# A small GpSimd step between any two indirect DMAs of a sorted-attention kernel

## The chip, the cores and the metric

The kernel runs on one core of one Trainium2 chip. A core has five engines that each work through a queue of their own, in order: PE (matrix products; its weight loads are shown apart as PEld), DVE (vector work), ACT (activation functions and copies), Pool (GpSimd: small general steps, and here every indirect DMA) and SP, which only issues DMAs. Engines wait for each other and for DMAs through semaphores.

The metric is the time of one execution on the device in microseconds (us), the median of several runs.

## The reference

Clustered attention over 4 batches, 8 heads, 768 tokens and a head size of 64, and behind it a small feed-forward network (FFN) over the 3072 tokens. A query attends only to the keys whose nearest of 16 centroids is its own nearest:

```python
q_assign = np.argmax(np.einsum('bhsd,hcd->bhsc', q_n, c_n), axis=-1)
k_assign = np.argmax(np.einsum('bhsd,hcd->bhsc', k_n, c_n), axis=-1)
mask = q_assign[:, :, :, None] == k_assign[:, :, None, :]
scores = scale * np.matmul(q, k.transpose(0, 1, 3, 2))
scores = np.where(mask, scores, -1000000000.0)
...
out = np.matmul(softmax(scores), v)

x = out.transpose(0, 2, 1, 3).reshape(B * S, H * D)
h = np.maximum(np.maximum(x @ w1, x @ w2), x @ w3)
return h @ w_out
```

Here `q_n`, `k_n` and `c_n` are the vectors divided by their lengths; `w1`, `w2`, `w3` are 512 x 768 and `w_out` is 768 x 512.

## The kernel before

Since a query meets only the keys of its own cluster, the kernel sorts the tokens of each head by cluster and computes attention in eight blocks of 128 places (`NJ = 8`, `NPLACE = 1024`). A place is a row of a buffer in DRAM, and the sorting of keys and values is done by DMA with computed addresses.

For each of the 32 heads (batch `b`, head `h`) the work goes through these steps:

- `four_units` (lines 367 to 493) finds clusters and places for four heads at a time: PE scores the centroids, DVE picks the best and counts, and the place of each token ends as an integer in the tile `cl_idx`.
- `split_kv` (line 548) makes 16-bit halves of keys and values in the tile `kv` (ACT at line 554, DVE at line 555).
- `scatter` (line 573) sends these rows to their places in a buffer in DRAM, one of a ring of four (`ring`, the name `kv_` in the code, `kv` in the profile). It takes six indirect DMAs, one for each 128 tokens, issued by Pool at line 578. No wait stands between the six, but each waits for the last readers of the ring's buffer.
- `read_back` (line 595) loads the sorted keys (a transposing DMA at line 602) and values (line 603) on SP's queue; they wait for all six scatters.
- `order_q` (line 615) sorts the queries on PE with products by 0/1 matrices: DVE builds `hot` at line 622, PE multiplies at line 624.
- `scores` (line 648) computes the blocks on PE and their exponentials on ACT (line 665), makes halves on DVE (line 670) and transposes them by DMA (line 672). `values` (line 678) multiplies with the values and writes the sorted result `of` to one of four buffers in DRAM (`oring`, the name `o`), with a DMA of SP at line 691.
- `gather` (line 693) brings the rows back in token order: six indirect DMAs of Pool at line 699 from `o` into `xb`, which holds one batch and has one buffer (`NXB = 1`). They wait for the write at line 691, and for `xb` to be free.

When the eight heads of a batch are gathered, `x_split` (line 713) makes halves of `xb` on ACT and DVE and transposes them by DMA into `x16`. The FFN of that batch (`ffn_units`, hidden products at line 741, output products at line 774) is spread over the steps of the next batch's heads. The FFN of the last batch has no next batch and runs alone at the end. The FFN weights are converted during the first twelve heads (`w_units`, `wo_units`).

The order is not written out by hand. Each piece of work gets a priority in `plan` (lines 792 to 863): for head number k, the scatter is put at k - 2.5, the read back at k - 1.5, the scores at k, the values at k + 0.5 and the gather at k + 1.6. When the program is built, a scheduler goes through the instructions with a time estimate of its own and fixes one order for each engine, so Pool's queue holds groups of six scatters and groups of six gathers. Behind the setup of tables and constants, Pool's queue holds nothing else.

Behind this program stands a second one, `every_pair__attn__then__maxout_ffn`, that runs only where the sorting does not fit its buffers. The profile has no work of it.

Of the kernel before, what the change touches and what calls it, by code (L numbers as in the profile page):

```python
# [8 lines left out]
F32 = mybir.dt.float32  # L9
# [6 lines left out]
ALU = mybir.AluOpType  # L16
# [7 lines left out]
def sorted_attn__then__maxout_ffn(  # L24
# [17 lines left out]
    nc = tc.nc  # L42
# [3 lines left out]
    P = 128  # L46
# [27 lines left out]

    def const(shape, dt, name):
        return cpool.tile(shape, dt, name=name)

    def after(x, o, why=mybir.DependencyReason.DATA):
        tc.add_manual_dep(
            x.ins, o.ins.name, mybir.DependencyInfo(mybir.DependencyClass.Sync, why), reason="one of several places"  # L80
        )


    ident = const([P, P], F32, "ident")
    make_identity(nc, ident)
    ident16 = const([P, P], BF16, "ident16")
    nc.gpsimd.tensor_copy(ident16, ident)
    identh = const([P, P], F16, "identh")
    nc.gpsimd.tensor_copy(identh, ident)
    cw = const([P, H, 2 * C], F32, "cw")  # L90
    nc.gpsimd.memset(cw, 0.0)

    def table(shape, name, *tests, dt=F16, fill=0.0):

        t = const([P] + shape, dt, name)
        nc.gpsimd.memset(t, 1.0)
        for free, part, base in tests:
            nc.gpsimd.affine_select(
                out=t, in_=t, pattern=[[f, n] for f, n in zip(free, shape)], compare_op=ALU.is_ge, fill=fill, base=base,
                channel_multiplier=part,  # L100
            )
        return t
# [27 lines left out]
    first = table([4, NJ, 4], "first", ([-2 * C, 0, 0], 1, 0), ([2 * C, 0, 0], -1, 2 * C - 1))  # L130
# [11 lines left out]
    side = const([P, 4], F32, "side")  # L142
# [356 lines left out]
    def pair_units(b, pr):  # L499
# [67 lines left out]
        def index(h, n, u):  # L567
            a = 2 * (2 * (pr & 1) + h) + u
            return fours[b, pr // 2]["idx"][:, n, a : a + 1]
# [3 lines left out]
        def scatter(h):  # L573
            def f():
                at = (2 * g + h) % NRING
                sent = d["sent", h] = []
                for n in range(QT):
                    i = nc.gpsimd.indirect_dma_start(  # L578
                        out=ring[at],
                        out_offset=bass.IndirectOffsetOnAxis(ap=index(h, n, 1), axis=0),  # L580
                        in_=d["kv", h][:, n].rearrange("p a d -> p (a d)"),
                        in_offset=None,
                        bounds_check=NPLACE - 1,
                        oob_is_err=False,
                    )
                    for o in sent:
                        tc.declare_no_dep(i.ins, o.ins, reason="each place is one token's")
                    for o in ring_last[at]:
                        after(i, o, mybir.DependencyReason.ANTI)
                    sent.append(i)  # L590
                ring_last[at] = []

            return f
# [99 lines left out]
    def gather(b, h):  # L693
        d, i = st[b, h // 2], h & 1
        od = oring[(b * H + h) % NOUT]
        if b not in xb:
            xb[b] = sb.tile([P, QT, DM], F32, tag="xb", name="xb", bufs=NXB)
        for n in range(QT):
            nc.gpsimd.indirect_dma_start(  # L699
                out=xb[b][:, n, h * D : h * D + D],  # L700
                out_offset=None,
                in_=od,
                in_offset=bass.IndirectOffsetOnAxis(ap=d["index"](i, n, 0), axis=0),
            )

    x16, xsc = {}, {}

# [125 lines left out]
    for b in range(B):  # L833
        for h in range(H):
            k = b * H + h
            put(k, when(k, k), scores, b, h)
            put(k + 1, when(k + 0.5, k), values, b, h)
            put(min(k + 1 + LATE, B * H), when(k + 0.6 + LATE, k), gather, b, h)
        k = b * H + H + LATE
        if b + 1 < B:  # L840
            put(k + 1, k - 0.5, x_scale, b)
            for n in range(QT):
                put(k + 1, k - 0.5 + 0.01 * n, x_split, b, n)
            units = [u for gi in range(NG) for u in ffn_units(b, gi)]
            spread(units, k + 1, k + H + 1 + (F2 if b == 2 else 0), 0)
# [778 lines left out]
```

## Time and profile before

| | before |
|---|---|
| median of 3 runs | 772.13 us (768.11 to 774.67) |
| the profiled execution, whole | 773.91 us |
| its span, first to last instruction | 772.2 us |
| mean granted TensorE clock | 0.885 of full |
| indirect DMAs | 192 scatters (L578), 192 gathers (L699) |

The span is what the views of the profile divide up; the execution has 1.7 us around it. L578 is line 578 of the kernel. A busy time counts only the time in which an engine works on an instruction; an engine's idle time ahead of an instruction is listed with what ended it, and `issue` stands for idle time in which the engine waited for nothing that the profile shows. For an indirect DMA the busy time is that of Pool, which makes the DMA's addresses, and not that of the transfer. Views group instructions by line and form (out<-in by names of tiles, partitions x elements, type), list the waits, or give the order of time.

The two groups of indirect DMAs are, with busy us, the mean ns of one, and the idle time ahead of them with what ended it:

```profile
L699 POOL DMA_INDIRECT xb<-o,cl_idx x192 | 195.5, 1018 | 132.8 <-DMA o<-of 70.5 <-issue 53.3 <-DVE xh L274 5.6
L578 POOL DMA_INDIRECT kv<-kv,cl_idx x192 | 212.5, 1107 | 85.0 <-issue 51.5 <-DVE kv L555 28.0 <-DMA xb<-o,cl_idx 0.9
```

Together Pool is busy with them for 408 us and idle ahead of them for 218 us, of which `issue` is 105 us.

### The profile page before, as it was taken

Reading aid. Unit: us, or ns where it says so; the run is one execution under the profiler, and the core shown is the slowest. Engines: PE = TensorE matmul, PEld = TensorE weight load, DVE = VectorE, ACT = ScalarE, POOL = GpSimd, SP = SyncE. Lnnn points to the kernel's source line nnn. Section 1 sums busy time; section 2 is a strip of 40 time slices with the busy share of each in tenths; the row PEclk is TensorE's granted clock in tenths of the full one; section 3 lists DMA queues with packets and bytes.
Section 4 is the critical chain, followed back from the end, with each engine's and each line's share of the span. In section 5 each row is a group of like instructions: output and inputs, shape, how many; then the busy total and the mean of one; then the engine's idle time right before and its main releaser. Section 6 shows DMA issues by size and latency. Waiting matters only on the chain.

```text
span 772.2 us, 12828 instructions
## 1 busy us (share of the span) xinstructions
PE 621.5 (80%) x4284; PEld 352.6 (46%) x4313; DVE 473.8 (61%) x1202; ACT 410.9 (53%) x978; POOL 426.4 (55%) x478
## 2 busy tenths in 40 slices
PE   3466446566527899999999998988799999999993
PEld 1233223334314465555455655644366465564651
DVE  4787867887588888586769765775554324121220
ACT  2567665977585666564867655565644413211111
POOL 6374577777765467777767575767276544000000
PEclk8579756557658899999999999999899999999998
DMA  9778879999699567898976656477845434200001
GB/s 319 272 214 188 224 179 221 271 220 255 180 265 184 138 144 204 172 217 172 215 172 162 130 135 176 118 154 138 163 90 113 120 77 84 69 1 28 14 1 46
DMA packets 231197, 120.54 MB, mean 156 GB/s; under 512 B 200656, under 2 KB 209872, under 8 KB 231120
## 3 DMA queue, kind: packets, MB, share of 16 engines
q1 hardware_dynamic: 218832, 100.72, 55.1%
q0 software_dynamic: 12288, 18.90, 9.7%
q8 instruction: 36, 0.59, 0.3%
q14 instruction: 41, 0.34, 0.1%
HBM read 58.75 MB, written 29.36 MB: 114 GB/s over the span
## 4 chain that ended last, share of the span: by engine, by line
PE 42%; DMA 15%; issue 13%; POOL 12%; DVE 9%; ACT 6%; SPq 2%; POOLq 0%; DVEq 0%; ACTq 0%
PE one L741 24%; PE one L774 9%; POOL kv L578 6%; POOL xb L699 5%; PE big L624 4%; DMA kv<-kv,cl_idx 4%; DMA xb<-o,cl_idx 3%; ACT e L665 2%; DMA o<-of 2%; DMA x<-xh 2%; DVE hot L622 2%; DMA wd<-in_moe_w_dram 1%; DVE kv L555 1%; DMA kt<-kv 1%; PE big L656 1%
## 5 line engine op out<-in xcount | busy, mean ns | idle before, releaser
L741 PE MATMUL one<-x,w 128*128 128x384 f16 x1728 | 296.6, 329 | 12.4 <-DVE wf_h L753 4.0
L699 POOL DMA_INDIRECT xb<-o,cl_idx x192 | 195.5, 1018 | 132.8 <-DMA o<-of 70.5
L578 POOL DMA_INDIRECT kv<-kv,cl_idx x192 | 212.5, 1107 | 85.0 <-issue 51.5
L741 PEld LDWEIGHTS <-w 128*128 128x128 f16 x1728 | 168.8, 99 | 126.7 <-issue 20.1
L624 PE MATMUL big<-hot,q 128*128 128x512 f16 x384 | 122.9, 442 | 47.9 <-DVE q L565 19.8
L665 ACT ACTIVATE e<-big,nm,sc_al 128x128 f32<-128x128 f32 x256 | 113.6, 462 | 29.2 <-DVE nm L661 16.2
L622 DVE TENSOR_SCALAR hot<-line,cl_code 128x1024 f16<-128x1024 f16 x192 | 92.3, 498 | 5.5 <-PE big L624 5.1
L624 PEld LDWEIGHTS <-q 128*128 128x128 f16 x384 | 37.6, 107 | 92.7 <-issue 46.9
L753 DVE SCALAR_TENSOR_TENSOR wf_h<-one,wf_h 128x384 f32<-128x384 f32 x48 | 26.6, 554 | 55.4 <-PE one L741 55.3
L753 DVE SCALAR_TENSOR_TENSOR vf_h<-one,vf_h 128x384 f32<-128x384 f32 x48 | 26.7, 555 | 51.0 <-PE one L741 51.0
L665 ACT ACTIVATION_READ_ACCUMULATOR e<-big,nm,sc_al 128x1 f32 x256 | 53.4, 209 | 0.0
L774 PE MATMUL one<-wo,wf_h 128*128 128x512 f16 x216 | 49.3, 386 | 1.5 <-ACT o L783 0.8
L774 PE MATMUL one<-wo,vf_h 128*128 128x512 f16 x216 | 48.7, 379 | 1.4 <-ACT o L783 1.4
L660 DVE TENSOR_REDUCE nm<-big 128x8 f32<-128x1024 f32 x32 | 39.0, 1217 | 16.0 <-PE big L658 8.6
L684 PE MATMUL one<-vt,pt 128*128 128x64 f16 x256 | 29.5, 203 | 21.3 <-DMA pt<-hl 18.9
L632 ACT CAST qt<-big 128x1024 f16<-128x1024 f32 x32 | 32.5, 1014 | 22.0 <-PE big L624 17.0
L783 ACT ACTIVATE o<-one,so 128x512 f32<-128x512 f32 x24 | 15.9, 685 | 51.4 <-PE one L774 40.0
L515 ACT ACTIVATE junk<-rows 128x768 bf16<-128x768 f32 x32 | 27.0, 843 | 30.1 <-DVE cl_code L467 20.0
L670 DVE SCALAR_TENSOR_TENSOR hl<-e,hl 128x1024 f16<-128x1024 f32 x32 | 38.9, 1214 | 5.4 <-ACT hl L669 5.3
L554 ACT ACTIVATE kv<-rows,sc_s 128x384 f16<-128x384 f32 x64 | 35.8, 613 | 8.7 <-DVE sc_s L542 8.7
L689 DVE TENSOR_TENSOR of<-one,r 128x512 f32<-128x512 f32 x32 | 21.9, 685 | 29.6 <-PE one L686 27.5
L555 DVE SCALAR_TENSOR_TENSOR kv<-rows,sc_s,kv 128x384 f16<-128x384 f32 x64 | 37.5, 611 | 2.8 <-ACT kv L554 2.7
(212 smaller groups left out, 890.3 us busy)
## 6 DMA issues: line engine op xcount, KB each, us to landing
stage<-in_qk_dram SPq DMA_DIRECT2D x32, 384.0 KB
wd<-in_moe_w_dram SPq DMA_DIRECT2D x18, 512.0 KB
vt<-kv SPq DMA_DIRECT2D x32, 256.0 KB
o<-of SPq DMA_DIRECT2D x32, 256.0 KB
rows<-in_kr_dram SPq DMA_DIRECT2D x16, 384.0 KB
rows<-in_v_dram SPq DMA_DIRECT2D x16, 384.0 KB
rows<-in_qr_dram SPq DMA_DIRECT2D x16, 384.0 KB
out_dram<-o SPq DMA_DIRECT2D x24, 256.0 KB
```

Source lines behind the costliest of these rows:

```text
L554: nc.scalar.activation(kv[:, :, at], x, AF.Copy, scale=s[:, i : i + 1])
L555: nc.vector.scalar_tensor_tensor(kv[:, :, at + 1], x, s[:, i : i + 1], kv[:, :, at], op0=ALU.mult, op1=ALU.subtract)
L578: i = nc.gpsimd.indirect_dma_start(out=ring[at], out_offset=bass.IndirectOffsetOnAxis(ap=index(h, n, 1), axis=0), in_=d["kv", h][:, n].rea ...
L622: nc.vector.tensor_scalar(a, line, code, None, op0=ALU.is_equal)
L624: nc.tensor.matmul(t[:, lo : lo + 512], d["q16"][:, h * QT + n].rearrange("p a d -> p (a d)"), a[:, lo : lo + 512], start=(n == 0), stop=( ...
L660: nc.vector.tensor_reduce(nm, ts, axis=AX.X, op=ALU.max)
L665: nc.scalar.activation(x[:, j], ts[:, j], AF.Exp, bias=nm[:, j : j + 1], scale=d["al"], accum_out=sm[:, j : j + 1])
L670: nc.vector.scalar_tensor_tensor(hl[:, 1], x, 2.0**14, hl[:, 0], op0=ALU.mult, op1=ALU.subtract)
L699: nc.gpsimd.indirect_dma_start(out=xb[b][:, n, h * D : h * D + D], out_offset=None, in_=od, in_offset=bass.IndirectOffsetOnAxis(ap=d["inde ...
L741: nc.tensor.matmul(t[:, 0:NB], w16[:, jt, wa, i, ct], x16[b, gi][:, :, xa * CT + ct, :], start=(n == 0), stop=(n == 3 * CT - 1),)
L753: nc.vector.scalar_tensor_tensor(m, t[:, 0:NB], 2.0**-23, ms[jt], op0=ALU.mult, op1=ALU.max)
L774: nc.tensor.matmul(t[:, 0:DM], h16[jt][:, ha, tt * P : (tt + 1) * P], wo16[:, jt, wa, :], start=(n == 0), stop=(n == 3 * JT - 1),)
```

## The change

A tile `blank` of 128 x 4 is made, and a function `spaced`. Behind each indirect DMA, of `scatter` and of `gather`, `spaced` has Pool multiply the constant tile `side` by itself into `blank`, which nothing reads. `keep_in_program_order` ties an instruction behind the one of the same engine that the program named just before it: it fixes the order in the queue and adds no wait. The step is tied behind its DMA, and the second to sixth DMA of a group are tied behind the step of the DMA before. The first DMA of a group is not tied, so the groups can still be set in any order. All in all 384 steps are added and nothing is taken away.

```diff
@@ -74,6 +74,14 @@
+    blank = const([P, 4], F32, "blank")
+
+    def spaced(i, first):
+
+        if not first:
+            tc.keep_in_program_order(i)
+        tc.keep_in_program_order(nc.gpsimd.tensor_tensor(blank, side, side, op=ALU.mult))
 
     def after(x, o, why=mybir.DependencyReason.DATA):
@@ -587,6 +595,7 @@
                     for o in ring_last[at]:
                         after(i, o, mybir.DependencyReason.ANTI)
+                    spaced(i, n == 0)
                     sent.append(i)
@@ -696,12 +705,13 @@
         for n in range(QT):
-            nc.gpsimd.indirect_dma_start(
+            got = nc.gpsimd.indirect_dma_start(
                 out=xb[b][:, n, h * D : h * D + D],
                 out_offset=None,
                 in_=od,
                 in_offset=bass.IndirectOffsetOnAxis(ap=d["index"](i, n, 0), axis=0),
             )
+            spaced(got, n == 0)
```

## The prediction

> **What bounds the kernel now.** I read the page's busy shares first, then the busy digits by slice, then a table by stage, then Pool's waits stage by stage, then the order of time around single instructions.
>
> ```profile
> span 772.2 us, 12828 instructions
> PE 621.5 (80%) x4284; PEld 352.6 (46%) x4313; DVE 473.8 (61%) x1202; ACT 410.9 (53%) x978; POOL 426.4 (55%) x478
> ...
> PE   3466446566527899999999998988799999999993
> ...
> POOL 6374577777765467777767575767276544000000
> ```
>
> No engine is full over the whole span. PE is at nine tenths from the second third on, and Pool is busy only up to 650 us. A table by stage, cut where Pool's pattern changes, says more (columns: stretch, then busy us and instruction count of each engine, the granted TensorE clock, the DMA share, GB/s):
>
> ```profile
> core 0: us, PE busy (x) PEld busy (x) DVE busy (x) ACT busy (x) POOL busy (x), PEclk, DMA share, GB/s
> 36.00:84.00 48.00, 27.90 (x181) 13.86 (x183) 39.63 (x107) 32.57 (x74) 26.98 (x25) 0.82 0.81 219
> 84.00:217.00 133.00, 77.39 (x531) 43.38 (x537) 99.97 (x272) 92.31 (x219) 103.75 (x96) 0.64 0.88 221
> 217.00:288.00 71.00, 52.95 (x351) 30.05 (x355) 59.57 (x171) 49.48 (x120) 38.09 (x37) 0.80 0.81 173
> 288.00:394.00 106.00, 102.25 (x791) 59.49 (x795) 77.74 (x191) 67.62 (x171) 81.78 (x78) 1.00 0.91 200
> 394.00:545.00 151.00, 135.14 (x1005) 80.00 (x1012) 103.67 (x254) 90.54 (x227) 97.50 (x91) 0.98 0.64 145
> 545.00:650.00 105.00, 102.27 (x745) 60.24 (x748) 47.49 (x96) 41.73 (x108) 58.91 (x60) 0.98 0.50 105
> 650.00:772.20 122.20, 108.88 (x614) 59.76 (x611) 24.88 (x45) 21.67 (x39) 0.82 (x1) 0.97 0.12 32
> ```
>
> Behind 36 us Pool runs nothing but indirect DMAs, so its counts there are DMA counts. Pool's busy time hides a part of what a DMA costs it, as the order of time shows (start, length, and in brackets the idle time ahead of it):
>
> ```profile
> 86.42 0.94 POOL L699 DMA_INDIRECT xb<-o,cl_idx  x1 [0.30 <-issue]
> 87.67 0.94 POOL L699 DMA_INDIRECT xb<-o,cl_idx  x1 [0.30 <-issue]
> 88.92 0.95 POOL L699 DMA_INDIRECT xb<-o,cl_idx  x1 [0.30 <-issue]
> ```
>
> One gather comes every 1.25 us: 0.94 busy and 0.30 in which Pool waits for nothing the trace shows. The view of waits sums these gaps for 85 to 217 us (us in total, times, longest):
>
> ```profile
> POOL xb L699 <- issue: 14.0, 45, 0.6
> POOL kv L578 <- issue: 12.8, 42, 0.3
> ```
>
> Without the one of 0.6 that is (26.8 - 0.6) / 86 = 0.305 each, and the few gaps under other names are of the same length. With them, 84 to 217 us is full: 103.75 us busy and some 95 gaps (29.0) make 132.7 of 133.0. So in that stretch Pool sets the pace while PE is busy 77 of 133 us. In 288 to 394 Pool (81.8 + 78 x 0.305 = 105.6 of 106) and PE (102.25 of 106) are both full. Elsewhere Pool waits for others; its real waits, by stretch (217 to 288, then 394 to 545, then 545 to 650):
>
> ```profile
> POOL kv L578 <- DVE kv L555: 15.9, 2, 12.1
> POOL xb L699 <- DVE worow L322: 2.7, 1, 2.7
> ...
> POOL xb L699 <- DMA o<-of: 22.3, 6, 5.1
> ...
> POOL xb L699 <- DMA o<-of: 29.6, 5, 10.6
> POOL xb L699 <- DVE xh L274: 5.6, 1, 5.6
> ```
>
> That is slack of 18.6, 22.3 and 35.2 us. The first and the last gather of all:
>
> ```profile
> 83.73 1.12 POOL L699 DMA_INDIRECT xb<-o,cl_idx  x1 [14.01 <-DMA o<-of]
> 649.51 1.30 POOL L699 DMA_INDIRECT xb<-o,cl_idx  x1 [0.30 <-issue]
> ```
>
> Behind the last stands the last batch's FFN on PE, 122 us that begin when it has landed; what delays it delays the end.
>
> **The change part by part.** *Added:* 384 TENSOR_TENSOR of 128x4 f32 on Pool (192 scatters and 192 gathers, one behind each). The trace has that very form:
>
> ```profile
> 17.26 0.20 POOL L150 TENSOR_TENSOR s_x<-s_x,side 128x4 f32<-128x4 f32 x1
> 17.39 0.13 POOL L149 MEMSET s_x<- 128x1 f32 x2
> L150 POOL TENSOR_TENSOR s_x<-s_x,side 128x4 f32<-128x4 f32 x8 | 1.6, 198 | 0.3
> ```
>
> It takes 198 ns, but the next instruction starts 17.39 - 17.26 = 0.13 us behind its start. Nothing in the trace shows a compute step between two indirect DMAs, so c, what a step adds to the pitch of two DMAs, has to be bounded. Where does the 0.30 belong, behind a DMA or ahead of one? These rows tell (DVE's L555 releases the scatter):
>
> ```profile
> 259.29 0.62 DVE L555 SCALAR_TENSOR_TENSOR kv<-rows,sc_s,kv 128x384 f16<-128x384 f32 x1
> 260.18 1.00 POOL L578 DMA_INDIRECT kv<-kv,cl_idx  x1 [12.13 <-DVE kv L555]
> ```
>
> L555 ends at 259.91 and the scatter starts at 260.18, 0.27 us later, on a Pool idle for 12 us. So nearly all of the 0.305 is a DMA's own lead-in, and a step between does not remove it: at most 0.305 - 0.27 = 0.035 is saved. And the first DMA behind a long wait (1.00 above) is no shorter than the ones behind it. Lower end: 0.13 - 0.035 = 0.095 us.
>
> Upper end: the full 0.198, and a delay by DVE. Here are one stretched gather, what ran beside it, and the DVE groups that matter:
>
> ```profile
> 356.92 1.89 POOL L699 DMA_INDIRECT xb<-o,cl_idx  x1 [0.30 <-issue]
> ...
> 356.78 1.21 DVE L670 SCALAR_TENSOR_TENSOR hl<-e,hl 128x1024 f16<-128x1024 f32 x1
> 357.91 0.47 DVE L622 TENSOR_SCALAR hot<-line,cl_code 128x1024 f16<-128x1024 f16 x1
> ...
> L622 DVE TENSOR_SCALAR hot<-line,cl_code 128x1024 f16<-128x1024 f16 x192 | 92.3, 498 | 5.5 <-PE big L624 5.1
> L670 DVE SCALAR_TENSOR_TENSOR hl<-e,hl 128x1024 f16<-128x1024 f32 x32 | 38.9, 1214 | 5.4 <-ACT hl L669 5.3
> L555 DVE SCALAR_TENSOR_TENSOR kv<-rows,sc_s,kv 128x384 f16<-128x384 f32 x64 | 37.5, 611 | 2.8 <-ACT kv L554 2.7
> L565 DVE SCALAR_TENSOR_TENSOR q<-rows,sc_s,q 128x768 f16<-128x768 f32 x16 | 16.2, 1014 | 0.4 <-ACT q L564 0.4
> ```
>
> The gather took 1.89 in place of 0.94 while L670 and L622 ran. If each such DVE instruction held up a step until its end, a step coming at a random moment would lose the sum of count x length² / 2 over the 614 us of 36 to 650: L622 23.8, L670 23.6, L555 11.9, L565 8.2, together 67.5 / 614 = 0.11 us. Upper end: 0.198 + 0.11, rounded up to 0.35 for the smaller DVE groups left out. I take 0.13 (the start-to-start row is what a follower feels) and some two thirds of that delay, c = 0.20 us.
>
> [...]
>
> *What lies on the path.* From 36 to 69 us there are 24 scatters: only the first head's six delay anything (6c = 1.2), the others fall into Pool's 14 us wait ahead of the first gather. From 84 to 217: 95 DMAs with no slack, 95c = 19.0. From 217 to 288: 36c = 7.2 into waits of 18.6, nothing passes. From 288 to 394: 78c = 15.6, hardly any slack; but behind it come the waits of 394 to 545 (22.3, against its own 90c = 18.0) and 545 to 650 (35.2 against 60c = 12.0), where Pool waits for PE's results; whether they absorb the 15.6 hangs on whether PE, full in 288 to 394, has by then been held up itself. I take half, 7.8. The last gather group has five steps inside: 5c = 1.0. Sum: 1.2 + 19.0 + 7.8 + 1.0 = 29.
>
> *Pinned order.* No semaphore wait comes with it: the step reads `side`, which DVE writes once at the start (line 143), and writes a tile nobody reads. Behind each step only Pool's own queue stands: the next DMA, and through it the transposes and loads of L602/L603 and the x_split of a batch. SP's queue gets nothing new. The instructions leave in an order that the program makes from its own estimates, and 384 more of them may shift it; one group of six changing places with its neighbour is worth 6 x 1.25 = 7.5 us, in either direction.
>
> The profiled execution took 773.91 us in all for its span of 772.2; the median of the three runs is 772.13, 1.8 lower. 773.91 + 29 - 1.8 gives about 801; I say 800.
>
> **The rivals.** *Absorbed (about 772):* the step fits into the 0.30 gap, if that time is spent in issuing and not on the cores, or DVE, ACT and the DMA queues (0.88 of the time busy in 84 to 217) turn out to set the pace of that stretch too. For it: the gap is the same 0.30 behind every DMA. Against it: Pool's own time adds up to the whole stretch, and the lead-in of 0.27 stays after idling.
>
> *Faster (about 752):* the step takes the lead-in's place. Between compute steps the next starts before the last has ended (0.13 against 0.198). If a DMA behind a compute step started like that, the lead-in of 0.305 would vanish and the pitch fall by 0.305 - 0.13 = 0.17: 95 x 0.17 = 16 us in 84 to 217, and at most the 106 - 102 = 4 us that PE leaves in 288 to 394. It decides once the lead-in falls below 0.13. The 0.27 behind a release speaks against it.
>
> *Locks in full (about 855):* if every step also waits its turn and pays a lead-in of its own, c is near 0.4: 101c = 40, 78c with nothing recovered 31, 90c - 22.3 = 14, 5c = 2, less 1.8: 858 by these terms, less a few for the waits at 221 and 260. It needs a step to start 0.2 late on average; the steps of L150, beside short DVE work, show none of it.
>
> **How the numbers follow.** A measurement tells about 1% (7.7 us) from no change. Pool paces the first batch and the time rises by 10 to 68 us: 0.63. Absorbed, within 1%: 0.18. Faster: 0.12. Locks in full, beyond 840: 0.07. The forecast case's own range goes from c = 0.095 (9.6 + 3.7 + 0.5 = 14, or 784) to c = 0.35 (35 + 78c = 27 + 2 = 64, or 836). The range takes in the absorbed case below: 768 to 840. Slower 0.70, same 0.18, faster 0.12.
>
> **What would show it.** Pool gets a group of 384 TENSOR_TENSOR with a mean near 0.2 us, and start-to-start of two gathers in 84 to 217 rises from 1.25 to about 1.45 us. The first batch's gathers, done at 217 us now, end at about 237, and the last gather of all moves from 649.5 to about 678. Pool's waits for o<-of and L555 shrink. PE's tail stays 122 us. The forecast is wrong if the idle time ahead of a DMA drops well below 0.27, if the first batch ends no later, or if Pool's groups come in another order.

## The result, and the profile after

The changed kernel takes 815.9 us in the median of 4 runs (813.4 to 820.4), the kernel before 770.9 in 4 runs beside it (768.1 to 774.7). The ratio is 1.059, with a 95% interval of 1.052 to 1.065: slower by 45 us. The profiled run of the changed kernel took 813.4 us, with a span of 811.6.

The rows of its page that answer to those of before are the span, the busy shares, the busy digits by slice and the shares of the chain that ended last (PE had 42% and Pool 12% of that chain before):

```profile
span 811.6 us, 13221 instructions
PE 626.6 (77%) x4285; PEld 352.3 (43%) x4313; DVE 481.3 (59%) x1202; ACT 410.4 (51%) x978; POOL 529.4 (65%) x862
...
PE   3556665555433999997499999897699999999994
...
POOL 6475788887888588888877787878678856000000
...
PE 32%; POOL 24%; DMA 15%; issue 13%; DVE 8%; ACT 4%; SPq 1%; POOLq 0%; DVEq 0%; ACTq 0%
```

Pool's groups of instructions (busy us, mean ns of one, then idle time ahead and what ended it) and its waits (us, times, longest); lines have moved by 8 or 9, so L586 is the scatter and L708 the gather:

```profile
L586 POOL DMA_INDIRECT kv<-kv,cl_idx x192 | 206.8, 1077 | 68.6 <-issue 50.1 <-DVE kv L563 11.7 <-DVE hot L631 0.9
L708 POOL DMA_INDIRECT xb<-o,cl_idx x192 | 198.3, 1033 | 68.2 <-issue 24.1 <-DMA o<-of 23.7 <-DVE cl_idx L479 7.0
L84 POOL TENSOR_TENSOR blank<-side 128x4 f32<-128x4 f32 x384 | 106.1, 276 | 17.9
```

```profile
POOL xb L708 <- DMA o<-of: 23.7, 7, 7.2
POOL kv L586 <- DVE kv L563: 11.7, 2, 10.8
POOL xb L708 <- DVE cl_idx L479: 7.0, 1, 7.0
POOL xb L708 <- DVE xh L282: 4.7, 2, 3.4
```

The DMAs are as long as they were. The 384 steps are there, with a mean of 276 ns, and Pool's waits for o<-of and for the split keys have shrunk from 70.5 and 28.0 us to 23.7 and 11.7.

But the order of time (start, length, idle time ahead) shows a program that isn't the one the change describes:

```profile
84.06 1.00 POOL L586 DMA_INDIRECT kv<-kv,cl_idx  x1 [0.30 <-issue]
85.07 0.30 POOL L84 TENSOR_TENSOR blank<-side 128x4 f32<-128x4 f32 x1
85.52 1.00 POOL L586 DMA_INDIRECT kv<-kv,cl_idx  x1 [0.16 <-issue]
86.82 0.97 POOL L586 DMA_INDIRECT kv<-kv,cl_idx  x1 [0.31 <-issue]
88.10 0.98 POOL L586 DMA_INDIRECT kv<-kv,cl_idx  x1 [0.30 <-DMA rows<-in_qr_dram]
...
130.58 1.01 POOL L708 DMA_INDIRECT xb<-o,cl_idx  x1 [0.30 <-issue]
131.61 3.16 POOL L84 TENSOR_TENSOR blank<-side 128x4 f32<-128x4 f32 x6
134.92 1.19 POOL L708 DMA_INDIRECT xb<-o,cl_idx  x1
...
142.31 0.95 POOL L708 DMA_INDIRECT xb<-o,cl_idx  x1 [0.30 <-issue]
143.28 2.15 POOL L84 TENSOR_TENSOR blank<-side 128x4 f32<-128x4 f32 x8
145.57 0.96 POOL L708 DMA_INDIRECT xb<-o,cl_idx  x1
...
257.63 0.97 POOL L708 DMA_INDIRECT xb<-o,cl_idx  x1
...
689.22 0.96 POOL L708 DMA_INDIRECT xb<-o,cl_idx  x1
690.21 0.20 POOL L84 TENSOR_TENSOR blank<-side 128x4 f32<-128x4 f32 x1
```

Three things are to be seen. First, scatters follow each other without a step: of 170 pairs of scatters in a row, 159 have none between them, and of 170 pairs of gathers 5. The trace has a register MOVE of Pool's sequencer for each of the 192 scatters (they carry a bounds check) and none for the gathers. The program names that MOVE just ahead of its scatter, so `keep_in_program_order` ties the scatter behind the MOVE and not behind the step. No run tests this reading by itself, but the difference between scatters and gathers fits it. What "The change" says of the second to sixth DMA of a group is so for gathers alone. Second, the steps left over pile up ahead of gathers, six and eight of them in the rows above, 17 in the longest; 211 of the 384 stand in such piles of four or more. All steps write the one tile `blank`, and in the trace 383 of the 384 wait on the semaphore that Pool's own steps count up, though the tie itself adds no wait (none of the 384 DMAs waits on that semaphore). So they keep the order in which they were named, and an undisturbed pile takes 0.276 us for each. Third, the first gather of a head, which isn't tied, is set ahead of the other five of an earlier head. The queue of before held whole groups of six; this one begins with 24 scatters, 1 gather, 12 scatters, 6 gathers, 12 scatters, 18 gathers, 6 scatters, 2 gathers. The 48th gather, the end of the first batch, is the row at 257.63; the last gather of all is the row at 689.22.

### The profile page after: what moved, and what is told of

It reads as the page before. It is cut to its first block, busy times and chain, and to the rows that moved or that the text cites. A ratio compares the mean times of both kernels' runs of the same rounds, so it can differ in the third digit from the quotient of the medians.

```text
span 811.6 us, 13221 instructions
## 1 busy us (share of the span) xinstructions
PE 626.6 (77%) x4285; PEld 352.3 (43%) x4313; DVE 481.3 (59%) x1202; ACT 410.4 (51%) x978; POOL 529.4 (65%) x862
## 4 chain that ended last, share of the span: by engine, by line
PE 32%; POOL 24%; DMA 15%; issue 13%; DVE 8%; ACT 4%; SPq 1%; POOLq 0%; DVEq 0%; ACTq 0%
PE one L751 19%; POOL kv L586 11%; POOL xb L708 8%; PE one L784 7%; POOL blank L84 5%; DMA rows<-in_v_dram 3%; PE big L633 2%; DMA xb<-o,cl_idx 2%; ACT e L674 2%; DMA kv<-kv,cl_idx 2%; DMA kt<-kv 2%; DMA x<-xh 2%; DMA pt<-hl 1%; DVE hot L631 1%; DMA wd<-in_moe_w_dram 1%
## 5 line engine op out<-in xcount | busy, mean ns | idle before, releaser
L586 POOL DMA_INDIRECT kv<-kv,cl_idx x192 | 206.8, 1077 | 68.6 <-issue 50.1
L708 POOL DMA_INDIRECT xb<-o,cl_idx x192 | 198.3, 1033 | 68.2 <-issue 24.1
L84 POOL TENSOR_TENSOR blank<-side 128x4 f32<-128x4 f32 x384 | 106.1, 276 | 17.9
L633 PEld LDWEIGHTS <-q 128*128 128x128 f16 x384 | 38.0, 106 | 121.7 <-issue 82.3
L281 ACT ACTIVATE xh<-xb,xsc 128x512 f16<-128x512 f32 x24 | 17.2, 721 | 65.3 <-DMA xb<-o,cl_idx 55.2
L282 DVE SCALAR_TENSOR_TENSOR xh<-xb,xsc,xh 128x512 f16<-128x512 f32 x24 | 18.0, 749 | 50.4 <-ACT xh L281 45.7
L665 PE MATMUL big<-kt,qt 128*128 128x128 f16 x256 | 25.9, 245 | 19.5 <-DMA kt<-kv 17.7
```

The lines of the kernel that those rows point to most:

```text
L84: tc.keep_in_program_order(nc.gpsimd.tensor_tensor(blank, side, side, op=ALU.mult))
L586: i = nc.gpsimd.indirect_dma_start(out=ring[at], out_offset=bass.IndirectOffsetOnAxis(ap=index(h, n, 1), axis=0), in_=d["kv", h][:, n].rea ...
L633: nc.tensor.matmul(t[:, lo : lo + 512], d["q16"][:, h * QT + n].rearrange("p a d -> p (a d)"), a[:, lo : lo + 512], start=(n == 0), stop=( ...
L708: got = nc.gpsimd.indirect_dma_start(out=xb[b][:, n, h * D : h * D + D], out_offset=None, in_=od, in_offset=bass.IndirectOffsetOnAxis(ap=d ...
```

## The experiments

Every kernel below computes everything. "Planned" says that the scheduler chose the order of the other engines anew; "held" says that TensorE, VectorE, ScalarE, SyncE and GpSimd were each tied to exactly the order of before. How far a planned kernel keeps the sequence of before can be counted in the traces, with like instructions (same line, tiles and form) taken in turn: the longest selection that stands in the order of before holds 81% of TensorE's, 57% of VectorE's and 81% of ScalarE's instructions in the changed kernel, and 80, 57 and 80% in before_order_steps. In same_order_steps_c it holds 99% or more of each.

This table is put together from the traces: the ends of the four batches of gathers (us from the span's start), Pool's waits over 0.6 us ahead of its DMAs, and Pool's own time, which is the last of the four ends less these waits. The medians are from runs on one chip (the first two rows' aside), where before took 770.2 and 770.8.

| kernel | median us | batches of gathers end at | Pool's waits | Pool's own time |
|---|---|---|---|---|
| before | 770.9 | 217.6, 369.2, 522.0, 650.8 | 106.8 | 544.0 |
| changed | 815.9 | 258.6, 423.9, 581.0, 690.2 | 50.2 | 640.0 |
| before_order_steps (planned) | 814.3 | 240.1, 404.2, 563.7, 691.4 | 77.6 | 613.8 |
| after_order_steps (planned) | 807.0 | 259.5, 421.0, 576.5, 684.8 | 70.9 | 613.9 |
| after_order_none (planned) | 777.8 | 239.6, 390.1, 545.9, 656.4 | 109.7 | 546.7 |
| before_order_memset (planned) | 784.9 | 224.4, 388.0, 542.8, 664.4 | 110.8 | 553.6 |
| same_order_steps_c (held) | 803.5 | 239.1, 395.7, 551.1, 679.5 | 67.8 | 611.8 |
| same_order_memset_c (held) | 769.7 | 215.8, 364.4, 518.0, 645.4 | 98.5 | 546.9 |

### First set: the steps, or Pool's order

Two theories stood against each other: the steps' own time makes the loss, or the order of Pool's DMAs does. In all four kernels a chain of ties writes out Pool's DMA order by head, and where there is a step, it stands truly behind its DMA (the diff is against the changed kernel, `...` marks what is left out; S3 stands for the six scatters of head 3, G3 for its gathers, and x1 or x5 for one or five of the six):

```diff
+    blank = const([P, 4, 4], F32, "blank")
+    def spaced(i, first, kind, head):
+        sent_by.setdefault((kind, head), []).append(i)
+        if kind in "SG":
+            at = 0 if kind == "S" else 1 + head % 3
+            steps[i.ins.name] = nc.gpsimd.tensor_tensor(blank[:, at], side, side, op=ALU.mult)
+    ORDER = (
+        "S0 S1 S2 S3 G0 S4 S5 G1 S6 S7 G2 G3 G4 S8 ..."
+    )
```

**before_order_steps:** the DMA order of before, with a step behind each of the 384 DMAs. The steps write four places in turn.

> Pool's DMAs in the order of the kernel before, one step truly behind each of the 384 DMAs. If the steps' own time makes the loss: 800 us by the forecast's sum, up to 816, with the pitch of two DMAs up by 0.15 to 0.25 us for scatters and gathers alike. If the loss comes from the order into which the DMAs fell (the first gather of a later head ahead of the rest of an earlier one): 771 to 780 us.

It took 814.3 us (ratio 1.055, 1.050 to 1.061).

**after_order_none:** the DMA order of the changed kernel, no steps (against the run before).

```diff
-            steps[i.ins.name] = nc.gpsimd.tensor_tensor(blank[:, at], side, side, op=ALU.mult)
...
-        "S0 S1 S2 S3 G0 S4 S5 G1 S6 S7 ..."
+        "S0 S1 S2 S3 G0x1 S4 S5 G1x1 G0x5 S6 S7 ..."
```

> Pool's DMAs in the order of the changed kernel, no step at all. If the order makes the loss: 795 to 816 us. If the steps' time makes it: within 1% of before, 764 to 779 us. If both: between.

It took 777.8 us (ratio 1.008, 1.005 to 1.012). So without the steps, Pool's order and the new orders that came with it on the other engines cost 7.6 us together, and the theory of the order alone falls. The first batch ends 22.0 us later than in before, the third 23.9 and the last 5.6: in the new order twelve more scatters stand ahead of the end of the first batch (132 DMAs in place of 120) and twelve fewer behind the third (60 in place of 72), so most of that delay is work moved ahead.

**after_order_steps:** the DMA order of the changed kernel, one step behind each DMA, so no piles.

> Pool's DMAs in the order of the changed kernel, one step truly behind each DMA in place of none between scatters and up to 17 in a pile ahead of a gather. If the piles (some 2.3 us each ahead of a gather) matter by themselves: well under 816, about 805. If only the number of steps and the order matter: 812 to 822 us.

It took 807.0 us (ratio 1.045, 1.039 to 1.051), less than before_order_steps: the two causes don't add up in these kernels.

**before_order_memset:** the DMA order of before, and a memset of the same 128x4 elements as the step (against before_order_steps).

```diff
-            steps[i.ins.name] = nc.gpsimd.tensor_tensor(blank[:, at], side, side, op=ALU.mult)
+            steps[i.ins.name] = nc.gpsimd.memset(blank[:, at], 0.0)
```

> As the first of these runs, but the step is a memset of 128x4, which reads nothing and whose follower starts 0.03 us behind its start in the setup. If a step costs its own length and DVE's hold on its reads: 775 to 785 us, clearly under the run with the product. If a step costs what it costs by standing between two DMAs at all, or through a new order on the other engines: as much as the run with the product.

It took 784.9 us (ratio 1.016, 1.011 to 1.021), although the median distance of two gathers stayed at 1.26 us. (The 0.03 us of the expectation is what the setup's memsets of 128x1 show, L149 of before; none of 128x4 stands there.) A step that adds nothing to the pitch of the DMAs cost 14.7 us. Pool's order was that of before, so what remained were the other engines, whose orders the scheduler had planned anew. The set had not kept them apart from the steps.

### Second and third set: orders held, on other chips

These kernels hold all five engines to the order of before, by ties written from that order (`traced` has the engine's instructions as the program names them, `at` their places in the order of before); the step goes behind its DMA.

```diff
+        for engine, text in ORDER.items():
+            at = np.cumsum(...)
...
+            last = None
+            for k in at:
+                for x in (traced[k], steps.get(traced[k].name)):
...
+                        tc.add_manual_dep(x, last.name, ..., reason="order")
+                    last = x
```

**same_order_steps** has the product behind each of the 384 DMAs, **same_order_memset** a memset, **same_order_S** the product behind scatters alone, **same_order_G_product** the product behind gathers and a memset behind scatters.

> Every engine, not Pool alone, keeps the order of the kernel before; one step behind each of the 384 DMAs. What is left is the steps' own time. If the whole loss is theirs: 812 to 817 us, as with Pool's order alone held. If new orders on PE, DVE and ACT have a share of some 15 us in it, as the memset run (784.9 us at an unchanged pitch of the DMAs) suggests: about 800 us.

> The same with a memset of 128x4 as the step. If the 14.7 us of the memset run came from the new orders on the other engines: 768 to 774 us, no change from before. If a memset costs by itself: 782 to 787 us.

> Every engine in the order of before, the product behind each of the 192 scatters, nothing behind the gathers. If each step counts alike: half of the loss of the run with all steps. If scatters run ahead of need and hide their steps in Pool's waits for results: less than a third of it.

> Every engine in the order of before, the product behind each of the 192 gathers and a memset behind each scatter. With the run before it this should add up to the run with all products if a memset is free; more than half of the loss if the gathers are the ones on the path.

On this chip the kernel before itself took 953.0 us in the median (937 to 969), 24% more than on the first, at a granted TensorE clock of 0.82 to 0.84, where the first chip's runs of before have 0.885 to 0.916. The four took 890.9, 966.4, 926.9 and 941.2 us. The first and the second were run again with nothing changed:

> The same kernel as same_order_steps, since that set ran where the kernel before itself took 953 us. If the whole loss is the steps' own time: 812 to 817 us against a before of about 770. If new orders on PE, DVE and ACT have a share of some 15 us in it: about 800 us.

> The same kernel as same_order_memset, repeated for the same reason. If the 14.7 us of the memset run with Pool's order alone held came from new orders on the other engines: 766 to 774 us. If a memset costs by itself: 782 to 787 us.

The third chip was like the second: before 951.3, steps 891.4 (ratio 0.932, 0.924 to 0.939; on the second chip 0.946, 0.940 to 0.953), memset 968.9 (1.020, 1.008 to 1.032). The products made the kernel faster there. The view of waits of same_order_memset_b shows Pool waiting for the attention results three times as long as the same kernel does in the fourth set (66.3 us), and VectorE waiting with a releaser that the trace can't name:

```profile
POOL xb L797 <- DMA o<-of: 210.4, 22, 20.5
...
DVE hot L720 <- remote: 57.2, 16, 15.0
```

The distances between DMAs were nearly those of the first chip (median of two gathers 1.35 us with the product and 1.26 with the memset, there 1.37 and 1.26), so the steps cost Pool about what they cost elsewhere. The traces show where much of the longer time lies: the transposing DMA that reads a head's keys back starts 8.4 us (mean of 32 heads) behind Pool's last scatter in same_order_memset_b and 3.3 in same_order_memset_c; with the product it's 5.3 in same_order_steps_b and 2.4 in same_order_steps_c. The traces of the third chip also hold only 24 and 33% of the semaphore updates of the indirect DMAs, those of the fourth set 95 and 97%, counted against 16 for each DMA (in the trace of before 347 of the 384 show 16 and none shows more). What holds the read back up on these chips, and why a later Pool helps there, stays open. These two sets aren't compared with the others.

### Fourth set: the same two kernels where before takes 771 us

> A third set with the two kernels that hold every engine (TensorE, VectorE, ScalarE, SyncE, GpSimd) in exactly the order of before, so that only the steps are added: one product of 128x4 elements behind each of the 384 indirect DMAs. It is to be read only if the kernel before takes about 770 us on this chip, as in the first set. Theory A, the steps' own time is the whole loss: 812 to 817 us, as with the orders that were planned anew (814.3). Theory B, the planned orders of the other engines carried a share of about 15 us: 797 to 803 us. Theory C, on record, most of the steps' time from 288 us on goes into GpSimd's waits: 795 to 801 us, which reads like B; the ends of the batches tell them apart: under C the third batch of gathers ends no later behind the second than in before, under B it does. If the kernel before takes about 950 us, the pair isn't compared with the first set.

> The same held orders with a memset of 128x4 elements as the step, which fits into the lead-in of the next indirect DMA. Theory A: the pitch of the DMAs in the median is unchanged, and what the memset run cost with planned orders (784.9 against 770.2) is its own time at places where it doesn't fit: 782 to 787 us. Theory B: that cost came from the planned orders of the other engines: 766 to 774 us.

Before took 770.8 us here. The steps took 803.5 us (ratio 1.040, 1.031 to 1.049) and the memset 769.7 us (ratio 0.999, 0.996 to 1.002). Theory A, that the steps' own time is the whole loss of the first set, falls, and B holds, though 803.5 lies just above its 797 to 803: with Pool's DMA order and the steps unchanged, holding the other engines took away 10.8 us of before_order_steps and 15.2 us of before_order_memset. C holds beside B, all but 2.7 us: the third batch ends 29.2 us later than in before and the second 26.5, and the fourth, 28.7 later, adds nothing. These are the rows of same_order_steps_c that carry it (groups, waits, and the last gather in the order of time; here L675 is the scatter and L797 the gather):

```profile
L84 POOL TENSOR_TENSOR blank<-side 128x4 f32<-128x4 f32 x384 | 118.8, 309 | 7.7
```

```profile
POOL xb L797 <- DMA o<-of: 44.1, 10, 13.2
...
POOL kv L675 <- DVE kv L652: 18.7, 3, 11.3
```

```profile
676.97 0.97 POOL L797 DMA_INDIRECT xb<-o,cl_idx  x1
677.95 0.47 POOL L84 TENSOR_TENSOR blank<-side 128x4 f32<-128x4 f32 x1
678.57 0.97 POOL L797 DMA_INDIRECT xb<-o,cl_idx  x1
679.56 0.21 POOL L84 TENSOR_TENSOR blank<-side 128x4 f32<-128x4 f32 x1
```

Where before takes 771 us, no kernel tried was faster than it by more than its interval.

## Why the prediction was right, and where it was wrong

The forecast was 800 us with a range of 768 to 840, and 815.9 came. The direction and the main mechanism were right; one step failed, and the range was wide enough to hold its cost.

**The sum for the steps held within the noise, by terms that partly cancel.** It priced the change as described: a step behind each DMA, in the order of before. same_order_steps_c is that program, and since its DMAs stand in the order of before, each can be compared with itself. The first batch was to end at about 237 and ended at 239.1: the first gather of all, put 1.2 us later, came 3.5 later (87.25 against 83.73), and the stretch behind it grew by 18.0 in place of 19.0. The term of 7.8 us for 217 to 650 came out at 7.7, but not by the half that was assumed. The delay is 21.4 us at the last gather before 217, 16.5 at the first behind 288, 29.3 at the last before 394 and 29.1 at the last of all. So 288 to 394 passed on 12.8 of its 15.6, the waits behind it took up their own stretches' steps and nothing of that, and 4.8 came back between 217 and 288, where the sum had nothing (3.4 of them also in same_order_memset_c, so most of it isn't the steps' doing). The last gather was to start at about 678 and did so at 678.57, and the tail stayed (121.7 us, before 121.4). The sum was 29; the span grew from 772.2 to 801.3, by 29.1, and the medians by 32.7, of which the interval makes 24 to 37. That one trace meets the sum to 0.1 us is luck.

**The price c = 0.20 was near, but two errors in it cancel.** Pool's own time grew by 67.8 us over 384 steps, 0.177 each. The prediction let a step save at most 0.035 of the lead-in of 0.305; the idle time between a step and the next DMA is 0.15 to 0.16 us, so it saves as much. By the prediction's own test ("the idle time ahead of a DMA drops well below 0.27") this was a mistake. Against it, VectorE held the steps up by more than the two thirds of 0.11 that were taken: the mean step is 309 ns where an undisturbed one takes 206 to 214. An undisturbed step adds 0.076 behind a gather and 0.093 behind a scatter (median distance of the end of a DMA and the start of the next like it: 0.381 and 0.398 in place of 0.305). The rest, some 0.09 or half of the price, is about what the mean step is longer than an undisturbed one (0.309 - 0.21).

These rows show the delay, and that it ends with the VectorE instruction (same_order_steps_c, order of time, VectorE first):

```profile
359.53 1.23 DVE L768 SCALAR_TENSOR_TENSOR hl<-e,hl 128x1024 f16<-128x1024 f32 x1
...
358.50 0.21 POOL L84 TENSOR_TENSOR blank<-side 128x4 f32<-128x4 f32 x1
358.87 0.99 POOL L675 DMA_INDIRECT kv<-kv,cl_idx  x1 [0.16 <-issue]
359.88 0.93 POOL L84 TENSOR_TENSOR blank<-side 128x4 f32<-128x4 f32 x1
360.97 0.99 POOL L675 DMA_INDIRECT kv<-kv,cl_idx  x1 [0.16 <-DVE hl L768]
```

VectorE's L768 ends at 360.76, the step at 360.81, and the scatter starts 0.16 behind that. In the whole trace 23 of the 24 steps that began with or during an L768 were like this, and the 24th began just ahead of it (mean of all 809 ns, ending 54 ns behind it in the median). The 22 that began during L758, a reduction of what PE left in PSUM, took 214 ns.

**The step that failed is "Pinned order".** It said "No semaphore wait comes with it" and costed the order at nothing, with a group of six that changes places at 7.5 us "in either direction". The steps do wait, on each other, since they all write `blank`; the scatters aren't separated; and the scheduler planned all engines anew. The prediction read the helper's name as what it does, and didn't ask what stands just before a scatter in the program. In its place the runs show 815.9 - 803.5 = 12.4 us that belong not to the steps as described but to piles and orders. Three parts are measured, each in a setting of its own: piles and skipped pairs raise Pool's own time by 28 us over the spread steps (640.0 against 611.8), of which an unknown share falls into waits; the changed DMA order costs 7.6 us without steps; new orders on the other engines cost 10.8 and 15.2 us where only they differ. They overlap, and the changed kernel with piles and the other engines' orders held wasn't tried. So how the 12.4 us are split is open. Of the three signs of being wrong that the prediction named, two came in the changed kernel, the lead-in behind a step (0.15) and the order of Pool's groups. The delay also came at other places than forecast: the first batch ends 41.0 us later than in before, where the sum had 20, and the third 59.0, of which 19.6 are made up behind it, since the new order has twelve scatters moved ahead. That 815.9 lies in the range all the same is luck, since the range was drawn from bounds of c and not from the order.

**The rivals.** *Absorbed* is true of a memset and not of the product. Here are three rows of same_order_memset_c, order of time:

```profile
103.38 0.97 POOL L675 DMA_INDIRECT kv<-kv,cl_idx  x1 [0.19 <-issue]
104.33 0.13 POOL L84 MEMSET blank<- 128x4 f32 x1
104.65 0.97 POOL L675 DMA_INDIRECT kv<-kv,cl_idx  x1 [0.19 <-issue]
```

The scatters are 1.27 us apart, the memset lies wholly in what was lead-in, and the ratio is 0.999. *Faster* needed a lead-in below 0.13; it fell to 0.15, and the step's own length used that up. *Locks in full*, with c near 0.4, didn't come: the mean price in the changed kernel is 96.0 / 384 = 0.25 us, and what lies above 0.18 came with the piles, which the rival hadn't named. Two small sums are off: its terms give 859, not 858, and c = 0.095 gives 786, not 784.

## What to carry to other kernels

A tie "behind the instruction before" is only as good as what the program put there: after such a change, read the order of time and count the steps between the neighbours it was meant for before pricing it. A dummy instruction on a queue that sets the pace is to be priced by its distance to the next start and its delays by other engines, not by its mean length: the product cost Pool 0.177 us each, at a mean length of 0.309. Where it only has to be there, one that reads nothing is worth a trial: the memset was free with the orders held (ratio 0.999). And when a program is planned again as a whole, an edit on one queue brings new orders on all of them, worth 11 to 15 us here, so an experiment on a small edit should hold the other queues' orders fixed.

## What the runs showed of the hardware

- The lead-in of an indirect DMA hung on what stood ahead of it. It was 0.305 us behind another DMA, 0.15 to 0.16 behind the end of the product and 0.188 behind the memset (medians of the traces of the changed kernel and the fourth set). The memset's 0.12 us hid in it whole (two gathers 1.26 us apart, in before 1.25); the product's undisturbed 0.21 did not (0.076 us more behind a gather, 0.093 behind a scatter).
- Which VectorE instructions held up a Pool step hung on both. Of the steps that began while VectorE was at work, products (same_order_steps_c) were held to its end by L768 (two inputs in SBUF; mean 809 ns) and by L720, a 16-bit comparison with one (52 of 57 steps; median 278 ns, ending 46 ns behind it), but not by L852, which has an input in PSUM (15 steps, 215 ns). Memsets (same_order_memset_c) were not held by L768 (19, mean 121 ns), but were by L720 (43 of 56; mean 275 ns).
- Steps of Pool that wait on the one before them started 0.276 us apart in the undisturbed piles of the changed kernel; a product of the same size in the setup of before (L150) let a follower that doesn't wait for it start after 0.13 us.
